# FNet mixing gated by a GLU on one Trainium2 core: three chunks of the sequence product together, and two of four block sums made by accumulating DMAs

## The chip, the cores and the metric

The kernel runs on one core of one Trainium2 chip. The metric is the device time of one execution in microseconds (us). The kernel before takes 804.07 us, the median of three runs (803.95 to 806.35). All operands are float32 in HBM (the chip's memory); work is done in SBUF (128 partitions) and in eight banks of PSUM.

## The reference

What is computed, cut to what matters; x is 2048 x 512, F is 1792:

```python
xn = layernorm(x)
s = C_re @ (xn @ H_re.T) - C_im @ (xn @ H_im.T)    # real part of a DFT along both axes
g = silu((sigmoid(xn @ w_gate) * (xn @ w_up)) @ w_down)
return x + s * g
```

C is the 2048 x 2048 DFT matrix of the sequence, H the 512 x 512 one of the hidden axis, each given as a real and an imaginary part.

## The kernel before

**Arithmetic.** Every float32 operand is split in two: ScalarE (ACT) copies a rounded high part (line 118), VectorE (DVE) subtracts it from the operand and keeps the low part (line 123). `mm3` (line 66) then makes one product of three matmuls: high by high, high by low, low by high. Each large product is done block-wise with seven products in place of eight, numbered k = 1 to 7; products 5, 6, 7 and 4 take sums of blocks as operands.

**Units.** The program is a list of units. One unit of the sequence product is 12 matmuls of 128 x 128 by 128 x 512. At unit n the main loop (last lines of the kernel) first calls what was put down with `sooner(n, ...)`, then issues the loads that units n to n+5 need (`LOAD_AHEAD`), then makes the high and low parts that units n to n+2 need (`SPLIT_AHEAD`), then records the unit's matmuls (`run`), and then calls what was put down with `after(n, ...)`. Nothing is reordered behind this: every engine gets its instructions in the order in which the program writes them.

**Queues.** All loads into SBUF are issued by SyncE (SP, line 79). All stores and all accumulating transfers are issued by GpSimd (POOL): `f_raw` (line 275, a finished block of the sequence product), `f_sum` (line 666, sums of such blocks), `g_part` (lines 479 and 482; line 479 accumulates in HBM), and `out`. Each queue starts its transfers in order; one instruction that waits holds up those behind it. A transfer is nearly always one page of 512 KB; SBUF holds 54 pages.

**The sequence stage.** The 2048 columns of the result fall into four chunks t of 512. In each chunk the contraction over the 2048 rows goes in four steps pp, so one product of one chunk is four units, and a chunk is 28 units; all four are 112 units (n = 112). On the x side the operands are blocks of the normalised x (`xs`, from `fetch`, `stats`, `normalise`) and sums of them (`a_sums`). `stats` runs two BN_STATS and two BN_AGGR on DVE, adds epsilon, and lets POOL take the power -1/2 (lines 164 to 173). On the DFT side each (t, pp) has four 512 KB blocks b11, b12, b21, b22 (the second index is the part, real or imaginary), and needs t1 = b11 + b12 for product 5, t2 = t1 + b22 for 6, t3 = b12 + b22 for 7 and t4 = t2 + b21 for 4. All four sums are made by DVE, in place (`onto`, `combine`, line 127), three units before their product; their blocks are loaded six units before it (`add_product`, line 308).

Chunks 0 and 1 go together through products 1 and 2: units 0 to 15 alternate between the two chunks, so that one block of x serves two units. Units 16 to 23 are chunk 2's products 1 and 2. Then come 5, 6, 7, 3, 4 of chunk 0 (units 24 to 43), of chunk 1 (44 to 63) and of chunk 2 (64 to 83), and chunk 3 as a whole (84 to 111). The sums of products grow in PSUM as chains "a", "b", "c" of two banks each (`CHAIN`); after product 1 its sum is copied by ACT into the banks of chain "b", and chain "a" goes on to products 6, 7 and 4.

**The start.** `begin` (line 349) records 12 matmuls on a tile of ones, loads the first block of x as two transfers of 256 KB, and makes the first operands by halves. For this first block alone the power is taken for each half as soon as its statistics are there (lines 167 and 168); for the others once per block (line 171).

**What else runs in the sequence stage.** `put_x` (line 699) lets POOL copy x into `out` (HBM to HBM), in units 40, 48, 56, ... ; `f_sums` (line 653) loads finished blocks of the first two chunks back, adds them on DVE and stores the sums, a first set from unit n-46 = 66 on and a second from n-35 = 77 on; `x_norm` and `x_ops` prepare the next stage.

Of the kernel before, what the change touches and what calls it, by code (L numbers as in the profile page):

```python
# [21 lines left out]
NT = S // 512  # L22
# [10 lines left out]
def fnet_glu_kernel(ctx: ExitStack, tc: tile.TileContext, x, x_t, c_re, c_im, w_h, w_gu, w_down, out):  # L33
# [112 lines left out]

    xs, mvs = {}, {}

    def fetch(j, pp, es=(0, 1)):
        if (j, pp) not in xs:  # L150
            xs[j, pp] = page([2, D], F32)
        rows = x[pp * SB : (pp + 1) * SB, :].rearrange("(p j e) d -> p j e d", j=2, e=2)[:, j]
        if len(es) == 2:
            nc.sync.dma_start(xs[j, pp], rows)
        else:
            nc.sync.dma_start(xs[j, pp][:, es[0], :], rows[:, es[0], :])

    def stats(j, pp):
        mv = stat.tile([P, 2, 2], F32, name="mv")
        rs = stat.tile([P, 2], F32, name="rs")  # L160
        mean, scale, bias = (moments[:, pp, m, j, :] for m in range(3))
        for e in range(2):
            st = stat.tile([P, 6], F32, name="st")
            nc.vector.bn_stats(st, xs[j, pp][:, e, :])
# [4 lines left out]
        if pp or j:  # L169
            nc.vector.tensor_scalar(rs, mv[:, :, 1], EPS, None, op0=ALU.add)  # L170
            nc.gpsimd.tensor_tensor(scale, rs, mhalf, op=ALU.pow)
        nc.vector.tensor_scalar(mean, mv[:, :, 0], -1.0, None, op0=ALU.mult)
        nc.gpsimd.tensor_tensor(bias, mean, scale, op=ALU.mult)
        return mv

# [50 lines left out]

    class Chunk:


        def __init__(self, t, tags, again):  # L230
            self.t, self.tags, self.ps, self.s = t, tags, {}, {}
            self.op, self.total = {}, {}
            for pp in range(4):
                b = {(j, m): c_block(t, pp, j, m) for j in range(2) for m in range(2)}
                self.op[1, pp] = Parts([b[0, 0]], b[0, 0].load, [2, SB])
                self.op[2, pp] = Parts([b[1, 0]], b[1, 0].load, [2, SB])
                if again:
# [16 lines left out]
        def needs(self, k, pp):  # L254
            return [aop[k, pp], self.op[k, pp]]

        def run(self, k, pp):
            ch = CHAIN[k]
# [4 lines left out]
            if (k, pp) == (1, 0) and self.t < 2:  # L263
                order.sort(key=lambda v: v[1])
            split_up = self.t < 2 and k in (1, 2) and (self.t, k, pp) != (0, 1, 0)
            for lows in ((0, 1), (2,)) if split_up else ((0, 1, 2),):
                for d, e in order:
                    ws = [v[:, e, d * P : (d + 1) * P] for v in wv]
                    first, last = k in (1, 5) and pp == e == 0, pp == 3 and e == 1
                    mm3(self.ps[ch, d], ws, [v[:, e, :] for v in xv], first, last, k not in (1, 5), self.t == 1, lows)  # L270
            if pp == 3:
                self.done(k)

# [43 lines left out]
    def begin_seq():  # L317
        tags = ("a", "b", "pd"), ("c", "pd", "a"), ("b", "pd", "a"), ("c", "a", "pd")
        chunks = [Chunk(t, dict(zip("abc", tags[t])), t in (1, 2)) for t in range(NT)]
        for i, k in enumerate((1, 2)):  # L320
            for pp in range(4):
                for c in chunks[:2]:
# [10 lines left out]
        for k in (1, 2):  # L333
            chunks[2].add_product(k)
        for pp in range(4):
            m = 9 + 2 * pp
            after(m, lambda pp=pp: a_sums(pp, (1,)))
            after(m + 1, lambda pp=pp: a_sums(pp, (3,)))
            after(m + 2, aop[5, pp].get)
            after(m + 3, lambda pp=pp: a_sums(pp, (2,)))  # L340
            after(m + 4, lambda pp=pp: a_sums(pp, (4,)))
        for c in chunks[:3]:
            for k in (5, 6, 7, 3, 4):
                c.add_product(k)
        for k in (1, 5, 6, 3, 7, 2, 4):
            chunks[3].add_product(k)
        return chunks

    def begin(chunks):
        for i, tag in enumerate(("gb", "ub", "pd", "pd")):  # L350
            idle = bank(tag)
            for _ in range((4, 4, 2, 2)[i]):
                nc.tensor.matmul(idle, ones[:, :P], ones, start=True, stop=True)
# [8 lines left out]
        for n in (2, 3):  # L362
            units[n][0][1].load()
        fetch(0, 2)
        for n in (4, 5):
            units[n][0][1].load()
        a = aop[1, 0]
        both = page([2, 2, D // 2])
        a.at = both[:, 0], both[:, 1]
        c.at = page([2, SB]), page([2, SB])  # L370
        first = a_block(0, 0, 0)

        def normed(e):
            scale = moments[:, 0, 1, 0, e : e + 1]
            nc.vector.tensor_scalar(first[:, e], first[:, e], mv[:, e, 0:1], scale, op0=SUB, op1=ALU.mult)

        def high(parts, src, e):
            nc.scalar.activation(parts[0][:, e], src[:, e], AF.Copy)

        def low(parts, src, e):  # L380
            nc.vector.tensor_tensor(parts[1][:, e], src[:, e], parts[0][:, e].bitcast(F32), op=SUB)

        mv = stats(0, 0)
        high(c.at, raw.at, 0)
        normed(0)
        high(a.at, first, 0)
        low(c.at, raw.at, 0)
        low(a.at, first, 0)
        high(c.at, raw.at, 1)
        normed(1)  # L390
        high(a.at, first, 1)
        low(c.at, raw.at, 1)
        low(a.at, first, 1)
        units[1][0][1].high()
        stats(0, 1)
        units[1][0][1].get()
        units[2][0][1].get()
        normalise(0, 1, d=0)
        aop[1, 1].get()
        for pp in range(2):  # L400
            after(4 + pp, lambda pp=pp: normalise(0, pp, d=1))


    XK = {(0, 0): 1, (1, 0): 2, (0, 1): 0, (1, 1): 3}
# [420 lines left out]
    with tc.manual_schedule():  # L825
# [97 lines left out]
```

## Time and profile before

| | |
|---|---|
| median of three runs | 804.07 us |
| the profiled execution | 804.23 us |
| its span, first to last instruction | 802.4 us |
| granted TensorE clock, mean | 0.996 |
| PE (matmuls) busy | 790.3 us, 3468 instructions |
| DVE busy | 685.9 us, 894 instructions |
| ACT busy | 510.7 us, 776 instructions |
| POOL busy | 123.0 us, 162 instructions |
| moved by DMA | 174.72 MB, mean 218 GB/s |

How to read it: the span is what the profiler saw of one execution; the 1.8 us between it and the execution's time lie outside. Busy times are sums over instructions; an engine with 98% busy time is the one that sets the end, unless its instructions are slowed down. DMA shares are shares of the core's 16 DMA engines together. The granted clock tells which part of its full speed TensorE was allowed.

### The profile page before, as it was taken

The page shows a single profiled execution, that of the slowest core. Times are in us where ns is not written, and L with a number is a line of the kernel's source. Part 1 is how long each engine was busy: PE and PEld are TensorE (multiplying, and loading weights), DVE is VectorE, ACT ScalarE, POOL GpSimd, SP SyncE. Part 2 cuts the span into 40 slices and gives each one's busy share as a digit, 9 for nine tenths or more (in the row PEclk, how much of TensorE's full clock was granted, in tenths as well). Part 3 has the DMA queues.
Part 4 walks back from the last instruction along what each step waited for, and adds up shares of the span by engine and source line. Part 5 has one row for each costly group of instructions (what it writes and reads, how often), then busy time and mean ns, then how long its engine had stood idle before and what let it go on. Part 6 is the DMA issues. An engine that isn't in the chain of part 4 may idle for free.

```text
span 802.4 us, 9870 instructions
## 1 busy us (share of the span) xinstructions
PE 790.3 (98%) x3468; PEld 651.6 (81%) x3468; DVE 685.9 (85%) x894; ACT 510.7 (64%) x776; POOL 123.0 (15%) x162
## 2 busy tenths in 40 slices
PE   7999999999999999999999999999999999999997
PEld 5888888888878888888887887888888888888885
DVE  6898999878899798899999967869688898896956
ACT  4984565525434555677777866666577787888471
POOL 2430001000110000001211111222131111112201
PEclk9999999999999999999999999999999999999999
DMA  8954057297898335238976976799999798999996
GB/s 339 410 192 160 27 179 267 86 340 256 283 374 366 105 110 202 83 115 214 202 131 97 179 166 184 245 275 240 241 261 213 159 227 227 223 290 299 298 340 106
DMA packets 49329, 174.72 MB, mean 218 GB/s; under 512 B 5504, under 2 KB 5760, under 8 KB 49280
## 3 DMA queue, kind: packets, MB, share of 16 engines
q0 software_dynamic: 20320, 70.28, 39.8%
q1 hardware_dynamic: 28880, 103.76, 35.5%
q8 instruction: 27, 0.44, 0.2%
q14 instruction: 22, 0.18, 0.1%
q10 hardware_dynamic: 80, 0.07, 0.0%
HBM read 106.95 MB, written 70.80 MB: 222 GB/s over the span
## 4 chain that ended last, share of the span: by engine, by line
PE 85%; DVE 5%; DMA 4%; issue 4%; POOL 1%; ACT 1%; SPq 0%; POOLq 0%; ACTq 0%; DVEq 0%
PE pd L70 25%; PE ga L70 15%; PE ua L70 15%; PE gc L70 10%; PE uc L70 10%; PE gb L70 5%; PE ub L70 5%; DMA g_part<-page 2%; DVE page L127 2%; DVE page L123 1%; DMA page<-in_x_dram 1%; DMA f_raw<-page 1%; POOL g_part L479 1%; ACT page L118 0%; DVE page L574 0%
## 5 line engine op out<-in xcount | busy, mean ns | idle before, releaser
L123 DVE TENSOR_TENSOR page<-page 128x512 fp32r<-128x512 f32 (+1 forms) x384 | 348.8, 938 | 62.9 <-ACT page L118 60.8
L118 ACT ACTIVATE page<-page 128x512 fp32r<-128x512 f32 (+1 forms) x384 | 303.1, 829 | 148.3 <-DVE page L127 116.5
L70 PE MATMUL pd<-page 128*128 128x512 f32 (+1 forms) x984 | 238.3, 386 | 0.0
L70 PEld LDWEIGHTS pd<-page 128*128 128x128 f32 x984 | 183.2, 188 | 37.5
L127 DVE TENSOR_TENSOR page<-page 128x1024 f32<-128x1024 f32 (+2 forms) x252 | 204.7, 833 | 4.9 <-DMA page<-in_w_gu_dram 3.8
L70 PE MATMUL ga<-page 128*128 128x512 f32 x600 | 154.4, 391 | 4.3 <-ACT page L118 1.8
L70 PE MATMUL ua<-page 128*128 128x512 f32 x600 | 154.2, 391 | 0.0
L70 PEld LDWEIGHTS ga<-page 128*128 128x128 f32 x600 | 112.5, 188 | 30.3 <-ACT page L118 2.4
L70 PEld LDWEIGHTS ua<-page 128*128 128x128 f32 x600 | 113.3, 189 | 23.7
L479 POOL DMA_DIRECT2D g_part<-page x76 | 66.4, 874 | 275.8 <-ACT page L488 159.0
L70 PE MATMUL gc<-page 128*128 128x512 f32 x384 | 98.6, 389 | 0.0
L70 PE MATMUL uc<-page 128*128 128x512 f32 x384 | 98.4, 389 | 0.0
L488 ACT ACTIVATE page<-pd 128x512 f32<-128x512 f32 x140 | 81.7, 600 | 24.3 <-PE pd L70 17.0
L70 PEld LDWEIGHTS gc<-page 128*128 128x128 f32 x384 | 72.2, 188 | 15.5 <-DVE page L123 0.5
L70 PEld LDWEIGHTS uc<-page 128*128 128x128 f32 x384 | 72.1, 188 | 14.9
L70 PE MATMUL gb<-page 128*128 128x512 f32 x252 | 64.9, 390 | 0.4 <-DVE page L123 0.4
L70 PE MATMUL ub<-page 128*128 128x512 f32 x252 | 64.6, 389 | 0.0
L70 PEld LDWEIGHTS gb<-page 128*128 128x128 f32 x252 | 47.2, 188 | 10.6 <-DVE page L123 0.8
L70 PEld LDWEIGHTS ub<-page 128*128 128x128 f32 x252 | 47.3, 188 | 9.8
L275 POOL DMA_DIRECT2D f_raw<-page x16 | 8.7, 544 | 220.6 <-DVE page L287 146.8
L614 DVE TENSOR_TENSOR page<-page 128x512 f32<-128x512 f32 x28 | 19.3, 689 | 8.7 <-ACT page L611 7.9
L574 DVE TENSOR_TENSOR page<-page,pd 128x512 f32<-128x512 f32 x28 | 18.5, 684 | 6.9 <-PE pd L70 6.9
(90 smaller groups left out, 347.8 us busy)
## 6 DMA issues: line engine op xcount, KB each, us to landing
g_part<-page POOLq DMA_DIRECT2D x84, 512.0 KB, 6.7
page<-in_c_re_dram SPq DMA_DIRECT2D x48, 512.0 KB, 7.7
page<-in_c_im_dram SPq DMA_DIRECT2D x32, 512.0 KB, 6.2
page<-f_raw SPq DMA_DIRECT2D x28, 512.0 KB, 8.2
page<-in_w_gu_dram SPq DMA_DIRECT2D x22, 512.0 KB, 5.9
f_raw<-page POOLq DMA_DIRECT2D x16, 512.0 KB, 5.7
f_sum<-page POOLq DMA_DIRECT2D x16, 512.0 KB, 7.1
page<-f_sum SPq DMA_DIRECT2D x16, 512.0 KB, 12.4
```

The lines of the kernel that those rows point to most:

```text
L70: nc.tensor.matmul(ps, ws[w], ms[m], start=first and i == 0, stop=last and i == 2, skip_group_check=go_on)
L118: nc.scalar.activation(self.parts[0], self.raw, AF.Copy)
L123: nc.vector.tensor_tensor(lo, self.raw, hi.bitcast(F32), op=SUB)
L127: (engine or nc.vector).tensor_tensor(dst, a, b, op=op)
L275: nc.gpsimd.dma_start(f_raw[self.t][block], v)
L479: nc.gpsimd.dma_start(g_part[i], pg, accum_op=ADD)
L488: nc.scalar.activation(pg[:, o, :], po, AF.Copy, scale=float(sign))
L574: nc.vector.tensor_add(self.part[:, o, :], self.part[:, o, :], ps)
L614: nc.vector.tensor_mul(s[k][:, 0, :], s[k][:, 0, :], ps["u" + tag] if tag else s[k][:, 1, :])
```

## The change

- **Three chunks together** (`TOGETHER = 3`): units 0 to 23 alternate between chunks 0, 1 and 2, so that one block of x serves three units. Products 1 and 2 of these chunks share a chain "p"; product 1 is copied from PSUM to SBUF, and copied back two units before product 6 (`again`). `fetch`, `stats`, `normalise` and `a_sums` get new places to match. In all of these units the three passes of `mm3` run one after the other over the four (d, e), where before the first two went together.
- **t1 and t3 by DMA** (`Sum`): SP loads the first block into a page, and an accumulating DMA that POOL issues adds the second block in SBUF. Both are issued nine units before the product. A page that t1 was made in before held b11, which product 1 (chunks 0 and 3) could share; now it is a load of its own, and b12 is read twice. t2 and t4 stay with DVE, loaded six units ahead.
- **Powers by halves**: the first two blocks of x are prepared by halves (`prepare`): DVE adds epsilon for each half and POOL takes the power of it. The first block of x is loaded in one transfer. Three more matmuls on the tile of ones.
- **f_sums(0, 1)** from unit n-26 = 86 on, instead of n-35 = 77.

The transfers of DFT blocks go from 80 to 124: 92 plain ones of SP and 32 accumulating ones of POOL. By groups of eight units, in the order of issue (from the code):

| units | 0-7 | 8-15 | 16-23 | 24-31 | 32-39 | 40-47 | 48-55 | 56-63 | 64-71 | 72-79 | 80-87 | 88-95 | 96-103 |
|---|---|---|---|---|---|---|---|---|---|---|---|---|---|
| before, plain | 13 | 8 | 9 | 2 | 4 | 8 | 2 | 12 | 2 | 5 | 9 | 2 | 4 |
| after, plain | 13 | 9 | 9 | 5 | 8 | 8 | 3 | 8 | 5 | 6 | 8 | 6 | 4 |
| after, accumulating | 0 | 1 | 4 | 3 | 4 | 4 | 1 | 4 | 3 | 1 | 3 | 4 | 0 |

Cut to its core, the diff reads:

```diff
@@ stats @@
-            if pp == j == 0:
-                nc.gpsimd.tensor_scalar(rs[:, e : e + 1], mv[:, e, 1:2], EPS, None, op0=ALU.add)
+            if apart:
+                nc.vector.tensor_scalar(rs[:, e : e + 1], mv[:, e, 1:2], EPS, None, op0=ALU.add)
                 nc.gpsimd.tensor_tensor(scale[:, e : e + 1], rs[:, e : e + 1], mhalf[:, e : e + 1], op=ALU.pow)
...
+    class Sum(Load):
+        def __init__(self, a, b, shape):
+            super().__init__(a, shape)
+            self.more = b
+        def load(self):
+            if self.at is None:
+                super().load()
+                nc.gpsimd.dma_start(self.at, self.more, accum_op=ADD)
+            return self.at
+        get = load
...
+    TOGETHER = 3
@@ Chunk.__init__ @@
                 if again:
-                    b[0, 0], b[1, 0] = c_block(t, pp, 0, 0), c_block(t, pp, 1, 0)
-                b11, b12, b21, b22 = b[0, 0], b[0, 1], b[1, 0], b[1, 1]
-                t1 = Value([b11, b12], onto(b11.load, b12.load))
+                    b[1, 0] = c_block(t, pp, 1, 0)
+                b21, b22 = b[1, 0], b[1, 1]
+                t1 = Sum(c_re[t, 0, pp], c_im[t, 0, pp], [2, SB])
+                t3 = Sum(c_im[t, 0, pp], c_im[t, 1, pp], [2, SB])
                 t2 = Value([b22], onto(t1.get, b22.load))
-                t3 = Value([b22], onto(b12.load, b22.load))
@@ Chunk.run @@
-            split_up = self.t < 2 and k in (1, 2) and (self.t, k, pp) != (0, 1, 0)
-            for lows in ((0, 1), (2,)) if split_up else ((0, 1, 2),):
+            split_up = self.t < TOGETHER and k in (1, 2)
+            for lows in ((0,), (1,), (2,)) if split_up else ((0, 1, 2),):
@@ Chunk.done @@
-            if k == 1:
+            if k < 3 and self.t < TOGETHER:
+                v = self.snap(f"p{k}", "p")
+                if k == 2:
+                    self.put(0, v)
+            elif k == 1:
@@ add_product @@
-        def add_product(self, k, total=(6, 3)):
+        def add_product(self, k):
+            total = (9, 3) if k in (5, 7) else (6, 3)
             for pp in range(4):
                 m = len(units)
+                if (k, pp) == (6, 0) and self.t < TOGETHER:
+                    after(m - 2, self.again)
@@ begin_seq @@
-                m = 8 * i + 2 * pp
-                if m > 4:
-                    sooner(m - (6, 7)[i], lambda i=i, pp=pp: fetch(i, pp))
-                if m > 2:
-                    sooner(m - (4, 5)[i], lambda i=i, pp=pp: stats(i, pp))
-                    sooner(m - 2, units[m][0][1].get)
-                    sooner(m - 2, lambda i=i, pp=pp: normalise(i, pp))
+                m = TOGETHER * (4 * i + pp)
+                if i:
+                    sooner(m - 11, lambda pp=pp: fetch(1, pp))
+                    after(m - 8, lambda pp=pp: stats(1, pp))
+                    sooner(m - 5, lambda pp=pp: normalise(1, pp))
+                else:
+                    if pp > 1:
+                        after(m - 5, lambda pp=pp: stats(0, pp))
+                        sooner(m - 2, lambda pp=pp: normalise(0, pp, 0))
...
@@ begin @@
-            for _ in range((4, 4, 2, 2)[i]):
+            for _ in range((4, 4, 4, 3)[i]):
...
-        for e in range(2):
-            fetch(0, 0, (e,))
+        fetch(0, 0)
...
-        f_sums(0, 1, n - 35, 2)
+        f_sums(0, 1, n - 26, 2)
```

How it moves instructions, at two places. The first is POOL's queue where the finished blocks of chunk 2 are stored (`f_raw_99`, `f_raw_98`, `f_raw_97`; units 75, 79 and 83). Before, the rows there are these; `f_sum` are the stores of f_sums, `out_dram<-in_x_t_dram` those of put_x:

```order
L275 DMA f_raw_99<-page 128x1024
L666 DMA f_sum_108<-page 128x1024
L275 DMA f_raw_98<-page 128x1024
L666 DMA f_sum_109<-page 128x1024
L701 DMA out_dram<-in_x_t_dram 128x2x512
L666 DMA f_sum_110<-page 128x1024
L275 DMA f_raw_97<-page 128x1024
```

And now, where `page<-in_c_im_dram` at line 227 is the accumulating transfer of a `Sum` (here for chunk 3's product 5):

```order
L296 DMA f_raw_99<-page 128x1024
L227 DMA page<-in_c_im_dram 128x1024
L296 DMA f_raw_98<-page 128x1024
L227 DMA page<-in_c_im_dram 128x1024
L736 DMA out_dram<-in_x_t_dram 128x2x512
L227 DMA page<-in_c_im_dram 128x1024 x2
L296 DMA f_raw_97<-page 128x1024
L701 DMA f_sum_108<-page 128x1024
L701 DMA f_sum_109<-page 128x1024
```

The accumulating transfers stand behind stores that wait for a product's result, and the f_sum stores of the second set have moved behind the last store of chunk 2.

The second place is DVE's order in the first units, where low parts (line 123) alternate with the statistics of the next block of x. Before:

```order
L123 TENSOR_TENSOR page<-page 128x512
L164 BN_STATS st<-page 128x6
L165 BN_AGGR mv<-st 128x2
L164 BN_STATS st<-page 128x6
L165 BN_AGGR mv<-st 128x2
L170 TENSOR_SCALAR rs<-mv 128x2
L172 TENSOR_SCALAR moments<-mv 128x2
L123 TENSOR_TENSOR page<-page 128x1024 x2
```

And now, behind unit 4, where the statistics of two blocks meet:

```order
L160 BN_STATS st<-page 128x6
L161 BN_AGGR mv<-st 128x2
L166 TENSOR_SCALAR rs<-mv 128x2
L170 TENSOR_SCALAR moments<-mv 128x2
L160 BN_STATS st<-page 128x6
L161 BN_AGGR mv<-st 128x2
L160 BN_STATS st<-page 128x6
L161 BN_AGGR mv<-st 128x2
L166 TENSOR_SCALAR rs<-mv 128x2
L170 TENSOR_SCALAR moments<-mv 128x2
L123 TENSOR_TENSOR page<-page 128x1024 x2
```

Two blocks' statistics now stand together ahead of the low parts, where before one block's did.

More of the change, by code (lines that the diff above doesn't have):

```diff
@@ L147, in fnet_glu_kernel, with fetch, stats @@
     xs, mvs = {}, {}
-    def fetch(j, pp, es=(0, 1)):
-        if (j, pp) not in xs:
-            xs[j, pp] = page([2, D], F32)
+    def fetch(j, pp):
+        xs[j, pp] = page([2, D], F32)
         rows = x[pp * SB : (pp + 1) * SB, :].rearrange("(p j e) d -> p j e d", j=2, e=2)[:, j]
[L153 to L158, printed above, removed]
+        nc.sync.dma_start(xs[j, pp], rows)
+    def stats(j, pp, apart=None):
         mv = stat.tile([P, 2, 2], F32, name="mv")
@@ L165, in stats @@
             nc.vector.bn_aggr(mv[:, e, :], st)
-            if pp == j == 0:
-                nc.gpsimd.tensor_scalar(rs[:, e : e + 1], mv[:, e, 1:2], EPS, None, op0=ALU.add)
+            if apart:
+                nc.vector.tensor_scalar(rs[:, e : e + 1], mv[:, e, 1:2], EPS, None, op0=ALU.add)
                 nc.gpsimd.tensor_tensor(scale[:, e : e + 1], rs[:, e : e + 1], mhalf[:, e : e + 1], op=ALU.pow)
-        if pp or j:
+        if not apart:
             nc.vector.tensor_scalar(rs, mv[:, :, 1], EPS, None, op0=ALU.add)
             nc.gpsimd.tensor_tensor(scale, rs, mhalf, op=ALU.pow)
+        if apart:
+            apart(mv, 0)
         nc.vector.tensor_scalar(mean, mv[:, :, 0], -1.0, None, op0=ALU.mult)
+        if apart:
+            apart(mv, 1)
         nc.gpsimd.tensor_tensor(bias, mean, scale, op=ALU.mult)
@@ L255, in needs, with again @@
             return [aop[k, pp], self.op[k, pp]]
+        def again(self):
+            self.chain("a")
+            for d in range(2):
+                nc.scalar.activation(self.ps["a", d], self.s["p1"][:, d, :], AF.Copy)
         def run(self, k, pp):
-            ch = CHAIN[k]
+            ch = "p" if k < 3 and self.t < TOGETHER else CHAIN[k]
             if k in (1, 5) and pp == 0:
@@ L262, in run @@
             order = [(d, e) for d in range(2) for e in range(2)]
[L263 removed]
+            if (k, pp) == (1, 0) and self.t < TOGETHER:
                 order.sort(key=lambda v: v[1])
[L265 to L266 removed]
+            split_up = self.t < TOGETHER and k in (1, 2)
+            for lows in ((0,), (1,), (2,)) if split_up else ((0, 1, 2),):
                 for d, e in order:
@@ L269, in run @@
                     first, last = k in (1, 5) and pp == e == 0, pp == 3 and e == 1
-                    mm3(self.ps[ch, d], ws, [v[:, e, :] for v in xv], first, last, k not in (1, 5), self.t == 1, lows)
+                    mm3(self.ps[ch, d], ws, [v[:, e, :] for v in xv], first, last, k not in (1, 5), self.t > 0 or (k < 3 and pp > 0), lows)
             if pp == 3:
@@ L317, in begin_seq @@
     def begin_seq():
-        tags = ("a", "b", "pd"), ("c", "pd", "a"), ("b", "pd", "a"), ("c", "a", "pd")
-        chunks = [Chunk(t, dict(zip("abc", tags[t])), t in (1, 2)) for t in range(NT)]
+        tags = {"p": "a", "c": "pd", "a": "a"}, {"p": "b", "c": "b", "a": "c"}, {"p": "c", "c": "pd", "a": "a"}, {"a": "c", "b": "a", "c": "pd"}
+        chunks = [Chunk(t, tags[t], t < TOGETHER) for t in range(NT)]
         for i, k in enumerate((1, 2)):
             for pp in range(4):
-                for c in chunks[:2]:
+                for c in chunks[:TOGETHER]:
@@ L331, in begin_seq @@
                 if i:
                     after(m + 2, lambda pp=pp: store_moments(pp))
-        for k in (1, 2):
-            chunks[2].add_product(k)
         for pp in range(4):
[L336 to L341, printed above, removed]
+            m = 4 * TOGETHER + TOGETHER * pp
@@ L342, in begin_seq @@
+            after(m - 3, lambda pp=pp: a_sums(pp, (1,)))
+            after(m - 2, lambda pp=pp: a_sums(pp, (3,)))
+            after(m - 1, aop[5, pp].get)
+            after(m + 1, lambda pp=pp: a_sums(pp, (2,)))
+            after(m + 5 + 2 * pp, lambda pp=pp: a_sums(pp, (4,)))
         for c in chunks[:3]:
@@ L361, in begin, with tile_of @@
         fetch(0, 1)
-        for n in (2, 3):
+        for n in (2, 3, 4):
             units[n][0][1].load()
         fetch(0, 2)
-        for n in (4, 5):
+        for n in (5,):
             units[n][0][1].load()
-        a = aop[1, 0]
-        both = page([2, 2, D // 2])
-        a.at = both[:, 0], both[:, 1]
         c.at = page([2, SB]), page([2, SB])
[L371 to L375, printed above, removed]
+        def tile_of(pp):
+            a = aop[1, pp]
+            both = page([2, 2, D // 2])
+            a.at = both[:, 0], both[:, 1]
+            return a.at, a_block(0, 0, pp)
@@ L377, in high, with normed, low @@
+        def normed(pp, mv, e):
+            v = a_block(0, 0, pp)[:, e]
+            nc.vector.tensor_scalar(v, v, mv[:, e, 0:1], moments[:, pp, 1, 0, e : e + 1], op0=SUB, op1=ALU.mult)
         def high(parts, src, e):
             nc.scalar.activation(parts[0][:, e], src[:, e], AF.Copy)
-        def low(parts, src, e):
+        def low(parts, src, e=slice(0, 2)):
             nc.vector.tensor_tensor(parts[1][:, e], src[:, e], parts[0][:, e].bitcast(F32), op=SUB)
-        mv = stats(0, 0)
-        high(c.at, raw.at, 0)
@@ L385, in begin, with prepare, step @@
[L385 to L395, printed above, removed]
+        def prepare(pp, between):
+            parts, src = tile_of(pp)
+            def step(mv, e):
+                normed(pp, mv, e)
+                high(parts, src, e)
+                between(e)
+            stats(0, pp, step)
+            return parts, src
@@ L396, in begin @@
+        high(c.at, raw.at, 0)
+        a, first = prepare(0, lambda e: high(c.at, raw.at, 1) if e == 0 else None)
+        for e in range(2):
+            low(c.at, raw.at, e)
+            low(a, first, e)
         units[1][0][1].get()
+        units[2][0][1].high()
+        a, second = prepare(1, lambda e: None)
+        units[3][0][1].high()
         units[2][0][1].get()
[L398 to L401, printed above, removed]
+        low(a, second)
```

3 lines of the change are left out of this document (added).

## The prediction

> **What bounds the kernel now.** I read the totals first, then the chain of work that ended last, then PE's waits, then the start and the stretch of the sequence stage row by row. Busy times by engine, and the chain's shares:
>
> ```profile
> span 802.4 us, 9870 instructions
> PE 790.3 (98%) x3468; PEld 651.6 (81%) x3468; DVE 685.9 (85%) x894; ACT 510.7 (64%) x776; POOL 123.0 (15%) x162
> PE 85%; DVE 5%; DMA 4%; issue 4%; POOL 1%; ACT 1%; SPq 0%; POOLq 0%; ACTq 0%; DVEq 0%
> ```
>
> PE is busy nearly always. The change adds three warm-up matmuls and takes no product away, so it can gain only what PE waits or runs slowly. These are all of PE's waits (us in total, times, longest):
>
> ```profile
> PE ga L70 <- ACT page L118: 1.8, 1, 1.8
> PE gb L353 <- DVE ones L50: 1.4, 1, 1.4
> PE ga L70 <- ACT page L378: 1.4, 1, 1.4
> PE ga L70 <- ACT page L596: 1.1, 2, 0.6
> PE gb L70 <- DVE page L123: 0.4, 1, 0.4
> ```
>
> Two lie at the start (L378, L118 at 1.8), L596 is in a later stage, and in the sequence stage beyond the start only 0.4 us remains, for DVE. Next the pace, from two rows of the chain of waits (start, duration):
>
> ```profile
> 37.59 2.72 PE pd L70 x12
> 67.50 21.76 PE pd L70 x96
> ```
>
> A unit of 12 matmuls takes 2.72 us. At 37.59 nine units are done, and 37.59 - 9 x 2.72 = 13.1; at 67.50 it is twenty, and 67.50 - 20 x 2.72 = 13.1 again. **So the start costs 13.1 us and from then on PE runs at its pace.** The start itself, in the timeline (start, duration, what, in brackets the wait ahead of it):
>
> ```profile
> 1.45 2.08 PE L353 MATMUL gb<-ones 128*128 128x512 f32 x4 [1.45 <-DVE ones L50]
> 5.03 1.91 PE L353 MATMUL pd<-ones 128*128 128x512 f32 x4
> 8.35 1.29 PE L70 MATMUL ga<-page 128*128 128x512 f32 x3 [1.42 <-ACT page L378]
> 12.40 1.68 POOL L171 TENSOR_TENSOR moments<-rs,mhalf 128x2 f32<-128x2 f32 x1 [4.18 <-DVE moments L172]
> 14.74 1.09 ACT L179 ACTIVATE page<-page,moments 128x256 f32<-128x256 f32 x2 [2.06 <-POOL moments L173]
> 16.54 1.25 PE L70 MATMUL ga<-page 128*128 128x512 f32 x4 [1.78 <-ACT page L118]
> ```
>
> The first product starts at 8.35. With two units per block of x, the second block is wanted at 8.35 + 2 x 2.72 = 13.8; its statistics, POOL's power and ACT's normalisation bring it at 16.54. One more thing costs here, the granted clock (busy time of PE, PEld, DVE, ACT, POOL, then clock, DMA share, GB/s):
>
> ```profile
> 17.00:21.00 4.00, 4.00 (x13) 3.10 (x12) 3.90 (x9) 1.39 (x2) 1.81 (x2) 0.57 1.03 420
> ```
>
> In these 4 us right behind the wait of 1.8 us the clock is 0.57: 4 x (1 - 0.57) = 1.7 us lost.
>
> **The change, part by part.**
>
> *32 DVE adds go.* Such an add, and the four stretches in which they lie:
>
> ```profile
> L127 DVE TENSOR_TENSOR page<-page 128x1024 f32<-128x1024 f32 x92 | 111.5, 1218 | 0.2 <-DMA page<-in_c_im_dram 0.2
> 60.00:110.00 50.00, 50.00 (x223) 41.39 (x222) 46.39 (x49) 31.50 (x42) 0.54 (x1) 1.00 0.25 84
> 110.00:160.00 50.00, 50.00 (x222) 41.42 (x221) 46.15 (x46) 24.62 (x30) 3.08 (x5) 1.00 0.56 203
> 160.00:200.00 40.00, 40.00 (x178) 33.10 (x178) 32.33 (x31) 14.96 (x17) 3.64 (x6) 1.00 0.84 302
> 200.00:227.00 27.00, 27.00 (x121) 22.36 (x120) 24.72 (x23) 11.13 (x12) 2.88 (x5) 1.00 0.79 275
> ```
>
> 32 x 1.218 = 39 us of DVE go. PE was busy in every microsecond of these rows, so this is worth nothing on the path; at most the 0.4 us of the one DVE wait.
>
> *The start.* Warm-ups: 12 take from 1.45 to 5.03 + 1.91 = 6.94, so 0.457 each; 15 end at 1.45 + 15 x 0.457 = 8.3. The first product cannot start before 8.35 either way, so they cost nothing. With three units per block the second block is wanted at 8.35 + 3 x 2.72 = 16.5 where 16.54 was reached before, and its power now goes by halves: **the 1.8 us wait goes, and with it the 1.7 us of slow clock**. What is late next: DVE. Its rows:
>
> ```profile
> 21.00:60.00 39.00, 39.00 (x173) 32.14 (x172) 36.65 (x65) 34.49 (x49) 14.67 (x17) 1.00 0.80 298
> L164 DVE BATCH_NORM_STATS2 st<-page 128x6 f32<-128x512 f32 x16 | 10.8, 677 | 3.8 <-DMA page<-in_x_dram 3.7
> L123 DVE TENSOR_TENSOR page<-page 128x1024 fp32r<-128x1024 f32 x182 | 219.4, 1218 | 34.0 <-ACT page L118 33.5
> L171 POOL TENSOR_TENSOR moments<-rs,mhalf 128x2 f32<-128x2 f32 x7 | 10.7, 1529 | 21.1 <-DVE moments L172 21.1
> ```
>
> DVE is busy 36.65 of 39 us there without holding PE. After the change two blocks' statistics stand together behind unit 4 (4 x 0.68 us and the small steps, estimated at half as much again: 4.1 us), ahead of low parts that are wanted two units later. Bounds for PE's wait there: 0 and 4.1; I take 1.2, since the lead of 5.4 us covers most of it. The blocks of units 9 to 16 need ACT and POOL's 1.53 us power in turn: 0 to 2.4, I take 1.2. The first unit, whose halves now come from one load, is stretched by 0.5 (0 to 1). Sum: 8.35 + 0.5 + 1.2 + 1.2 = 11.25 in place of 13.1, **a gain of 1.85 us**; by the bounds from 4.7 gained (nothing waits) to 2.7 lost, and a renewed slow clock would add 1.7.
>
> *What an accumulating transfer costs.* The traces show none into SBUF; the nearest row is g_part, which accumulates in HBM. The two queues, and what stands in them:
>
> ```profile
> q0 software_dynamic: 20320, 70.28, 39.8%
> q1 hardware_dynamic: 28880, 103.76, 35.5%
> L479 POOL DMA_DIRECT2D g_part<-page x76 | 66.4, 874 | 275.8 <-ACT page L488 159.0
> out_dram<-page POOLq DMA_DIRECT2D x7, 512.0 KB, 10.3
> 227.00:258.00 31.00, 30.62 (x135) 25.00 (x134) 30.18 (x28) 13.38 (x15) 4.64 (x8) 1.00 1.02 417
> ```
>
> At 0.524 MB a page q1 has 198 plain pages: 0.355 x 802.4 / 198 = 1.44 us of all 16 engines each. q0 has 134, of which 76 + 7 = 83 accumulate: (0.398 x 802.4 - 51 x 1.44) / 83 = 2.96 us each, 2.06 times a plain one. Where the engines are full (417 GB/s in the last row) a plain page takes 0.524 / 0.417 = 1.26 us, so 2.06 times that is 2.58. An add in SBUF may be cheaper: the lower bound is a plain page, 1.26; the upper 2.96. I take 2.58, nearest to the row.
>
> [...]
>
> *Where there is room for it.* Chunk 0's and 1's sixteen accumulating transfers and their extra loads fall into 60 to 160, where the DMA share is 0.25 and 0.56: 37.5 + 22 = 59 us free, against 16 x 2.58 = 41 and some 9 plain ones, 11 us. They fit. From 160 to 258 (units 54 to 90) the free time is 40 x 0.16 + 27 x 0.21 + 0 = 12.1 us. There the sum is, from the table by units: accumulating +12 (4 + 3 + 1 + 3 and one), plain ones unchanged (29 and 29), and of f_sums' second set two of its eight transfers move behind 258 (2.5 us). **12 x 2.58 - 12.1 - 2.5 = 16.4 us more work than room at 258.** What of it is covered:
>
> ```profile
> DMA to landing us min/median/max: 3.2/3.3/3.4
> 258.00:285.00 27.00, 27.00 (x121) 22.36 (x120) 22.45 (x21) 13.78 (x16) 0.00 (x0) 1.00 0.25 84
> ```
>
> The first row is SP's loads from 258 to 285, when the queues are empty: 3.3 us. Blocks for t2, t4 are loaded six units ahead, 16.3 us, so the cover is 16.3 - 3.3 = 13.0 us; the accumulating ones have more, 24.5 less their own time. So PE waits about **16.4 - 13.0 = 3.4 us**, around 255 to 275; after that the engines are 75% free and it is caught up. In order on POOL's queue, stores of finished blocks stand ahead of the accumulating ones, and f_sum's stores behind: nothing but the later f_sums waits for these. On DVE, t2's and t4's adds are queued ahead of low parts: a late load stops DVE and by it PE. That is the way in which the lack shows. By the bounds of the price, 12 x 1.26 leaves 0.5 us and no wait; 12 x 2.96 leaves 20.9 and a wait of 7.9.
>
> *The rest.* b11's extra loads are in the table. p1's copies to SBUF and back are ACT's (9 more instructions; ACT has 64% busy), hidden behind PE; cost nothing unless the chain is wanted within one unit, and `again` stands two units ahead.
>
> **Sum.** 804.23 (the profiled execution) - 1.85 + 3.4 = **805.8 us**; the median of the runs is 0.16 lower than that execution, which changes nothing.
>
> **The rivals.**
>
> A, the forecast: the start gains, the full DMA engines take it back. 805.8, own range 804 to 809.
>
> B: the accumulating transfers stay hidden. For it: SBUF is not HBM, and the cover of 13.0 us is lost only above (13.0 + 12.1 + 2.5) / 12 = 2.3 us each. Against it: the 2.58. Time: 804.23 - 1.85 = 802.4.
>
> C, slower: the price is 2.96 and the backlog decides. From 2.3 us on, each 0.1 us costs 1.2 us of waiting; at 2.96 it is 7.9 us, and as such a wait is longer than the 1.8 us behind which the clock fell to 0.57, it falls again: + 1.7. Time: 804.23 - 1.85 + 7.9 + 1.7 = 812.0. For it: 227 to 258 is already full at 1.02. Against it: the engines took 2.06 times, not 2.35.
>
> [...]
>
> D, slower: the start loses. The two statistics in a row hold PE for the whole 4.1 us and ACT's turn for 2.4, a wait over 1.8 us brings the slow clock: 8.35 + 0.5 + 4.1 + 2.4 + 1.7 = 17.1 in place of 13.1, with the transfers hidden 808.2. Against it: DVE at 36.65 of 39 held nobody.
>
> **How the numbers follow.** A 0.47, B 0.30, C 0.15, D 0.08. A measurement of this kernel can tell about 0.3%, 2.4 us. Same (801.7 to 806.5): three fifths of A, two thirds of B, 0.48. Faster: the rest of B and a start near its better bound, 0.14. Slower: the rest of A, C and D, 0.38. The range runs from below B, with a start that gains 3 us (801.2), to C (812.0); one tenth is left out on each side.
>
> **What will show it.** First unit at 8.35, no wait of 1.8 us ahead of the second block, granted clock 1.0 from 17 to 21, and 11.3 us lost when the pace is reached. DMA share near 1 from 160 to 270 in place of 0.84 and 0.79; PE's waits for L123 between 250 and 275, with DVE's L127 waiting for page<-in_c loads ahead of them. Wrong would be: free DMA time left in 200 to 227 (price too high), waits of PE at 60 to 160 (an engine other than these), or waits in the hidden stage, where no edit reaches.

## The result, and the profile after

The changed kernel takes 815.6 us, median of five runs (812.97 to 816.44), against 803.95 for the kernel before in the same session. The ratio is 1.0139, with a 95% interval of 1.0125 to 1.0154: **slower by 1.4%**. The forecast was 805.8 with a range up to 812.0. The profiled execution took 812.97 us, the quickest of the five, so what the trace shows is the least of the harm.

The totals after, and the two DMA queues:

```profile
span 811.2 us, 9964 instructions
PE 793.0 (98%) x3471; PEld 652.5 (80%) x3471; DVE 651.7 (80%) x867; ACT 512.0 (63%) x785; POOL 146.6 (18%) x193
q0 software_dynamic: 24928, 87.06, 50.0%
q1 hardware_dynamic: 30464, 110.05, 36.1%
```

DVE has lost 34 us of work, and the span has grown by 8.8. GpSimd's queue q0 went from 39.8% to 50.0%. PE's waits after (us in total, times, longest; those of the first products and of the later stage left out):

```profile
PE ga L70 <- DVE page L123: 4.8, 1, 4.8
PE pd L70 <- DVE page L123: 2.6, 1, 2.6
...
PE gb L70 <- DVE page L123: 1.2, 2, 0.8
```

Before, PE waited 0.4 us for DVE in the whole sequence stage; now it is two long waits and some at the start. By stretches (busy time of PE, PEld, DVE, ACT, POOL, then granted clock, DMA share, GB/s):

```profile
17.00:21.00 4.00, 4.00 (x19) 3.34 (x18) 3.90 (x9) 2.14 (x4) 1.37 (x1) 1.00 1.03 422
21.00:60.00 39.00, 37.43 (x160) 29.24 (x160) 31.70 (x56) 29.73 (x44) 12.84 (x17) 1.00 0.76 306
60.00:75.00 15.00, 15.00 (x68) 12.43 (x67) 13.76 (x18) 9.37 (x14) 3.33 (x5) 1.00 1.01 233
75.00:110.00 35.00, 35.00 (x156) 29.00 (x155) 28.80 (x33) 25.86 (x37) 5.94 (x8) 1.00 0.86 255
110.00:160.00 50.00, 50.00 (x222) 41.39 (x222) 37.55 (x37) 25.59 (x31) 10.04 (x13) 1.00 0.95 293
160.00:200.00 40.00, 40.00 (x178) 33.15 (x177) 26.03 (x25) 15.58 (x18) 7.79 (x11) 1.00 0.99 306
200.00:227.00 27.00, 22.23 (x89) 17.93 (x89) 15.18 (x15) 10.25 (x11) 3.95 (x7) 0.87 0.96 299
227.00:258.00 31.00, 31.00 (x138) 25.68 (x137) 23.00 (x21) 11.81 (x13) 5.74 (x8) 1.00 1.04 337
258.00:285.00 27.00, 24.42 (x102) 19.79 (x101) 22.79 (x20) 10.68 (x14) 6.36 (x9) 0.94 1.03 380
285.00:300.00 15.00, 15.00 (x68) 12.40 (x67) 10.51 (x10) 8.18 (x9) 0.56 (x1) 1.00 1.00 303
```

Read the DMA share first. Before, it was 0.25 from 60 to 110 and then, in the same stretches as here, 0.56, 0.84, 0.79, 1.02, 0.25 and 0.41; now it is 0.86 to 1.04 all the way from 60 to 300. Then PE: it is idle 1.57 us from 21 to 60 (the start), 4.77 from 200 to 227 and 2.58 from 258 to 285. Behind both of the later waits the clock is low (start, length, then the same columns):

```profile
218.50:223.00 4.50, 4.20 (x10) 3.33 (x11) 4.50 (x5) 3.90 (x4) 1.24 (x2) 0.50 0.71 218
264.00:268.00 4.00, 3.55 (x9) 2.85 (x10) 4.00 (x5) 0.00 (x0) 0.12 (x1) 0.57 1.03 421
```

That costs 4.5 x 0.50 = 2.2 us and 4 x 0.43 = 1.7 us more. **The two stops together take about 4.8 + 2.2 + 2.6 + 1.7 = 11.3 us.** The chain of waits agrees: unit 92, the first of a new product, starts there at 273.85, and 273.85 - 92 x 2.72 - 12.3 (lost at the start, next) = 11.3.

The start, from the row of the chain of waits that begins with unit 24:

```profile
77.58 10.88 PE pd L70 x48
```

77.58 - 24 x 2.72 = 12.3 us are lost before the pace is reached, 0.8 less than the 13.1 that the same view gave before.

What held PE in the two stops is told by DVE's waits and by the chain. DVE's two waits, first of the stretch 200 to 220, then of 226 to 266:

```profile
DVE page L123 <- DMA f_sum<-page: 9.4, 1, 9.4
...
DVE page L127 <- DMA page<-f_raw: 7.7, 1, 7.7
```

And the three longest links of the chain of waits from 180 to 270 (start, duration; a DMA from its issue to its landing):

```profile
188.69 14.90 DMA page<-in_c_im_dram
...
204.68 12.76 DMA f_sum<-page
...
240.74 21.20 DMA page<-f_raw
```

The first stop: a load of SP, the first block of a t3 (it comes from `in_c_im`), takes 14.9 us; its accumulating transfer waits 3.9 us for it at the head of POOL's queue; the f_sum store behind that starts at 204.68 and takes 12.8 us; and DVE, by the releaser that the profile names, waits 9.4 us for the landing of the store before it writes a low part (line 123). It waits for a store, so what it needs is the page that the store reads. The second stop: f_sums' load of a finished block, issued 240.74, takes 21.2 us, and DVE's add (line 127) waits 7.7 us for it, with low parts queued behind. In both cases the transfer that lands last belongs to f_sums. In the first stop another was nearly as late: the accumulated block of the stopped unit was sent for at 199.38 and landed 12.1 us later, and ACT waited 2.7 us for it before it could make the high part; PE stopped at 218.80 - 4.77 = 214.0.

### The profile page after: what moved, and what is told of

The parts are those of the page before. It is cut to its first block, busy times and chain, and to the rows that moved or that the text cites. A ratio compares the mean times of both kernels' runs of the same rounds, so it can differ in the third digit from the quotient of the medians.

```text
span 811.2 us, 9964 instructions
## 1 busy us (share of the span) xinstructions
PE 793.0 (98%) x3471; PEld 652.5 (80%) x3471; DVE 651.7 (80%) x867; ACT 512.0 (63%) x785; POOL 146.6 (18%) x193
## 4 chain that ended last, share of the span: by engine, by line
PE 84%; DMA 9%; DVE 2%; ACT 2%; issue 1%; POOL 1%; SPq 0%; DVEq 0%; POOLq 0%
PE pd L70 26%; PE ga L70 14%; PE ua L70 14%; PE uc L70 10%; PE gc L70 10%; PE gb L70 5%; PE ub L70 5%; DMA page<-in_c_re_dram 3%; DMA page<-f_raw 3%; DMA page<-in_c_im_dram 2%; DMA f_sum<-page 2%; ACT page L118 1%; DVE page L123 1%; ACT page L179 1%; POOL moments L167 0%
## 5 line engine op out<-in xcount | busy, mean ns | idle before, releaser
L123 DVE TENSOR_TENSOR page<-page 128x1024 fp32r<-128x1024 f32 (+1 forms) x383 | 346.8, 939 | 95.4 <-ACT page L118 80.6
L118 ACT ACTIVATE page<-page 128x1024 fp32r<-128x1024 f32 (+1 forms) x383 | 301.0, 830 | 139.4 <-DVE page L127 103.1
L127 DVE TENSOR_TENSOR page<-page 128x512 f32<-128x512 f32 (+2 forms) x220 | 165.8, 777 | 10.5 <-DMA page<-f_raw 7.7
L70 PE MATMUL gc<-page 128*128 128x512 f32 x408 | 106.6, 389 | 0.0
L70 PE MATMUL uc<-page 128*128 128x512 f32 x408 | 106.6, 389 | 0.0
L70 PEld LDWEIGHTS gc<-page 128*128 128x128 f32 x408 | 76.6, 188 | 15.9
L70 PEld LDWEIGHTS uc<-page 128*128 128x128 f32 x408 | 76.6, 188 | 15.9
L70 PEld LDWEIGHTS gb<-page 128*128 128x128 f32 x228 | 42.6, 188 | 10.9 <-DVE page L123 2.2
L70 PEld LDWEIGHTS ub<-page 128*128 128x128 f32 x228 | 42.8, 188 | 8.9
L227 POOL DMA_DIRECT2D page<-in_c_im_dram x32 | 28.3, 931 | 94.5 <-DMA page<-in_c_re_dram 25.2
## 6 DMA issues: line engine op xcount, KB each, us to landing
page<-f_raw SPq DMA_DIRECT2D x28, 512.0 KB, 11.3
```

Source lines behind the costliest of these rows:

```text
L70: nc.tensor.matmul(ps, ws[w], ms[m], start=first and i == 0, stop=last and i == 2, skip_group_check=go_on)
L118: nc.scalar.activation(self.parts[0], self.raw, AF.Copy)
L123: nc.vector.tensor_tensor(lo, self.raw, hi.bitcast(F32), op=SUB)
L127: (engine or nc.vector).tensor_tensor(dst, a, b, op=op)
L227: nc.gpsimd.dma_start(self.at, self.more, accum_op=ADD)
```

## The experiments

Three theories were set against each other. Theory 1: f_sums decides, because its loads are issued only three units (8.2 us) ahead. Theory 2: the DMA engines have more work than room, because an accumulating transfer holds them about twice as long as a plain one (1.94 times, as measured below); what is late first is an accident. Theory 3: POOL's queue decides, because an accumulating transfer waits for its first block (38.1 us of POOL's waits for loads ahead of line 227 in the changed kernel) and holds the stores behind it. All comparisons are with the kernel before, run again beside each.

### t1 and t3 by DVE again, all else as changed

```diff
-                    b[1, 0] = c_block(t, pp, 1, 0)
-                b21, b22 = b[1, 0], b[1, 1]
-                t1 = Sum(c_re[t, 0, pp], c_im[t, 0, pp], [2, SB])
-                t3 = Sum(c_im[t, 0, pp], c_im[t, 1, pp], [2, SB])
+                    b[0, 0], b[1, 0] = c_block(t, pp, 0, 0), c_block(t, pp, 1, 0)
+                b11, b12, b21, b22 = b[0, 0], b[0, 1], b[1, 0], b[1, 1]
+                t1 = Value([b11, b12], onto(b11.load, b12.load))
+                t3 = Value([b22], onto(b12.load, b22.load))
...
-            total = (9, 3) if k in (5, 7) else (6, 3)
+            total = (6, 3)
```

> The changed kernel with t1 and t3 made by DVE again, loaded six units ahead as before; the three chunks together, the powers by halves, the warm-ups and the later f_sums stay. If the accumulating transfers are the cause (theories 1, 2 and 3 below alike), PE's two stops at units 74 and 89 (7.0 and 4.3 us with the slow clock behind them) go and the start's gain of 0.8 us stays: 803.2. If three chunks together are the cause, the stops stay: 812 to 816.

803.5 us; ratio 0.9989 [0.9980, 0.9999]. The stops are gone; the rows where the changed kernel stopped, in this run:

```profile
200.00:227.00 27.00, 27.00 (x121) 22.36 (x120) 24.62 (x24) 11.69 (x13) 2.88 (x5) 1.00 0.80 281
258.00:285.00 27.00, 26.78 (x118) 21.85 (x117) 25.72 (x23) 14.30 (x16) 2.28 (x4) 1.00 0.47 156
```

So the accumulating transfers, with the loads that come with them, are the harm, and all the rest of the change together gains a tenth of a per cent.

### Only the accumulating transfers, in the kernel before

```diff
...
-                t1 = Value([b11, b12], onto(b11.load, b12.load))
+                t1 = Sum(c_re[t, 0, pp], c_im[t, 0, pp], [2, SB])
+                t3 = Sum(c_im[t, 0, pp], c_im[t, 1, pp], [2, SB])
...
-                t3 = Value([b22], onto(b12.load, b22.load))
...
-        def add_product(self, k, total=(6, 3)):
+        def add_product(self, k):
+            total = (9, 3) if k in (5, 7) else (6, 3)
```

> The kernel before with t1 and t3 by SP's load and the accumulating DMA nine units ahead, and nothing else of the change: two chunks together, start and f_sums as before. Theories 1 and 2 expect PE stops of 8 to 12 us between 200 and 280: 812 to 816; with f_sums' second set earlier (from unit 77) the stops come earlier and rather longer. If three chunks together are needed for the harm, 804.

816.02 us; ratio 1.0152 [1.0127, 1.0177]. This one edit does as much harm as the whole change. PE's waits for DVE after the start are here 3.4 and 1.8 us and some smaller ones; three chunks together are not needed for it.

### The same transfers without the add

The second transfer of a `Sum` becomes plain; it overwrites the first block, so t1 and t3 are not sums here.

```diff
-                nc.gpsimd.dma_start(self.at, self.more, accum_op=ADD)
+                nc.gpsimd.dma_start(self.at, self.more)
```

> The changed kernel with the accumulating transfers as plain ones: same queue, same waits, same bytes, but the second block overwrites the first, so t1 and t3 are not sums. Theory 1 (f_sums: its loads, three units ahead on a full DMA, stop DVE) and theory 2 (the price of the add on the DMA engines) expect 32 x (2.69 - 1.26) = 46 us less DMA work and no stop: 803 to 805. Theory 3 (POOL's queue: an accumulating transfer waits for its first block and holds the stores behind it) expects the stops as they are: 811 to 816.

803.58 us; ratio 0.9986 [0.9976, 0.9996]. The number of transfers, their queue, their order and their waits are those of the changed kernel, and no stop is left: the add itself is what harms. **Theory 3 falls**, as an explanation by itself. The stretch where the changed kernel stopped, in this run:

```profile
160.00:200.00 40.00, 40.00 (x179) 33.10 (x178) 27.89 (x27) 16.68 (x21) 6.25 (x11) 1.00 0.96 348
200.00:227.00 27.00, 27.00 (x121) 22.37 (x120) 20.27 (x20) 11.31 (x12) 3.92 (x7) 1.00 0.97 328
227.00:258.00 31.00, 31.00 (x138) 25.67 (x137) 22.89 (x21) 12.08 (x14) 5.19 (x10) 1.00 1.02 407
258.00:285.00 27.00, 27.00 (x120) 22.21 (x119) 22.87 (x22) 16.00 (x18) 3.75 (x7) 1.00 0.85 341
```

The shares are nearly as high, 0.96, 0.97 and 1.02, and PE is busy throughout. So a share near 1 is not by itself the harm; what the add costs on top is measured next.

### The price of the add by itself

Two runs of the kernel before with eight unused pages in the quiet stretch: a plain load of SP, and into the same page an accumulating or a plain transfer of POOL.

```diff
...
+        for i in range(8):
+            sooner(20 + 2 * i, Sum(c_re[3, 0, 0], c_im[3, 0, 0], [2, SB]).load)
```

> The kernel before with eight more pages that nothing uses, one every second unit from unit 20: a plain load of SP and an accumulating transfer of POOL into it, in the quiet stretch. It measures the price by itself. Before, the DMA engines were busy 0.25 x 50 = 12.5 us from 60 to 110; with a price of 2.58 (the forecast) they are busy about 12.5 + 8 x 1.3 + 8 x 2.58 = 43.5, with 2.96 about 46.6, with the cost of a plain transfer 33. No effect on the time if the units lie in the quiet stretch: 804.

> The same with eight plain transfers of POOL in place of the accumulating ones: 12.5 + 16 x 1.3 = 33 us busy from 60 to 110 by every theory. The difference between the two runs over eight is what the add costs on top of a plain transfer: 1.3 by the forecast's price, 1.2 by the totals of the changed kernel and its plain variant, 0 if the add is free in the quiet. The time 804.

The times were 803.56 and 803.23 us, beside 802.95 for the kernel before, one run each: next to nothing on the path. The row from 55 to 120, which holds all sixteen transfers, first of the kernel before:

```profile
55.00:120.00 65.00, 65.00 (x289) 53.81 (x288) 60.72 (x66) 39.00 (x52) 3.09 (x6) 1.00 0.40 134
```

with eight plain ones of POOL:

```profile
55.00:120.00 65.00, 65.00 (x288) 53.81 (x288) 60.74 (x66) 38.94 (x52) 7.28 (x14) 1.00 0.74 264
```

and with eight accumulating ones:

```profile
55.00:120.00 65.00, 65.00 (x288) 53.84 (x287) 60.70 (x66) 38.90 (x52) 10.00 (x14) 1.00 0.90 258
```

A plain page costs (0.74 - 0.40) x 65 / 16 = 1.38 us of all engines, the add (0.90 - 0.74) x 65 / 8 = 1.30 us on top: **2.68 us for an accumulating transfer into SBUF, 1.94 times a plain one.** The totals say nearly the same: q0 takes 46.0% of 800.7 us in the run with the second transfers plain and 50.0% of 811.2 in the changed kernel, 37.3 us for 32, or 1.17 each on top. From 60 to 110 the expected 43.5 us came out as 0.91 x 50 = 45.5, and the 33 of the plain run as 0.69 x 50 = 34.5.

### Loads of f_sums six and nine units ahead

```diff
...
-        f_sums(0, 0, n - 46, 2)
-        f_sums(0, 1, n - 26, 2)
+        f_sums(0, 0, n - 46, 2, 6)
+        f_sums(0, 1, n - 26, 2, 9)
```

The last argument is the lead of its loads, which was three.

> The changed kernel with the blocks for f_sums loaded six and nine units ahead of their adds instead of three; no transfer more or less. Theory 1 expects the second stop (4.3 us with the slow clock behind it, DVE's add waiting for a block that takes 21.2 us to land) to go: 4 us faster than the changed kernel, about 811.5. Theory 2 expects another late block in its place and 814 to 817. On the first stop, where a page is held by a store of f_sums, both expect little change.

812.96 us; ratio 1.0106 [1.0089, 1.0123], by the two ratios 0.3% better than the changed kernel, some 2.6 us. This time lies between what the theories expected, 811.5 by theory 1 and 814 to 817 by theory 2, and does not decide; the trace does. The first stop is nearly as long and comes earlier; the chain there reads:

```profile
184.97 6.87 DMA page<-in_c_im_dram
...
193.02 12.04 DMA f_raw<-page
...
205.14 1.06 ACT page L118
```

Now it is the store of a finished block that holds a page, and ACT's high part (line 118) that waits. The second stop breaks into pieces:

```profile
200.00:227.00 27.00, 22.89 (x93) 18.11 (x92) 15.21 (x14) 11.02 (x12) 4.30 (x7) 0.94 0.99 316
227.00:258.00 31.00, 29.44 (x129) 23.80 (x128) 20.51 (x20) 11.27 (x12) 5.14 (x7) 1.00 1.03 352
258.00:285.00 27.00, 25.97 (x113) 20.59 (x112) 24.52 (x22) 12.34 (x16) 6.39 (x9) 1.00 1.03 362
```

PE is idle 4.11 + 1.56 + 1.03 = 6.7 us in these rows, against 4.77 + 2.58 = 7.4 in the changed kernel; the rest of the gain goes with the clock, which was slow for less time (0.94 and 1.00 from 200 to 227 and from 258 to 285, in place of 0.87 and 0.94). In one of the pieces DVE's add waits 1.5 us for a block from `in_c_im`, loaded by SP, which takes 22.9 us to land: the sort of wait that the prediction had in mind. So **theory 1 falls in its strict form**: with f_sums served early, other transfers take its place, as theory 2 says.

### f_sums in other places

Its second set back at unit 77, as before the change:

```diff
-        f_sums(0, 1, n - 26, 2)
+        f_sums(0, 1, n - 35, 2)
```

> The changed kernel with the second set of f_sums back at unit 77. No transfer more or less. Theory 2 (the add's price fills the DMA engines from 60 to 300 us; whichever transfer is then wanted soonest stops DVE) expects the second stop earlier and no smaller: 813 to 818. Theory 1 (the cover of the f_sums loads decides, wherever the engines are full) expects the same here.

816.33 us; ratio 1.0152 [1.0128, 1.0176]. The stops stay (5.2 and 2.3 us of waiting for line 123), the second 11 us earlier. Both theories expected as much, so this run does not part them; the place of f_sums within the full stretch matters little.

Both early sets out of the stretch:

```diff
-        f_sums(0, 0, n - 46, 2)
-        f_sums(0, 1, n - 26, 2)
+        f_sums(0, 0, n + 4, 2)
+        f_sums(0, 1, n + 14, 2)
```

> The changed kernel with both early sets of f_sums moved out of the full stretch, to units 116 and 126 (330 us on, where the DMA share is low). The 32 accumulating transfers stay. Theory 2 by its budget: the plain variant needed 119 us of engine time from 160 to 285, the adds bring 16 x 1.17 = 19 us more, the f_sums moved out take 16 x 1.3 = 21 us away: 117 of 125, no stop, 803 to 805. Theory 1 expects the same, since the loads with short cover are gone; but if other loads stop DVE the time stays above 808 and both fall.

808.24 us; ratio 1.0049 [1.0035, 1.0063]. No stop, but not the 803 to 805 that both theories expected; the rows of this run where the changed kernel stopped, and the one where f_sums now runs:

```profile
200.00:227.00 27.00, 27.00 (x121) 22.36 (x120) 16.77 (x17) 11.16 (x13) 1.46 (x2) 1.00 0.80 251
227.00:258.00 31.00, 31.00 (x139) 25.66 (x138) 21.58 (x20) 12.81 (x15) 5.01 (x7) 1.00 1.04 345
258.00:285.00 27.00, 27.00 (x121) 22.36 (x120) 19.65 (x19) 15.28 (x18) 3.47 (x4) 1.00 0.79 229
...
300.00:360.00 60.00, 57.87 (x253) 46.93 (x252) 55.07 (x75) 34.59 (x56) 4.80 (x9) 1.00 0.58 206
```

With 16 transfers fewer in the stretch PE is never idle there, as the budget of theory 2 had it. Most of the gain is given back later: PE waits 3.8 us in all for line 631 of ACT, against 0.5 in the changed kernel, and 1.9 of it lies between 300 and 360, where f_sums now runs. That the moved f_sums cause these later waits is likely by their place; it was not tried.

### Half of the accumulating transfers

t1 by DMA, t3 by DVE with a load of b12 of its own.

```diff
...
-                t3 = Sum(c_im[t, 0, pp], c_im[t, 1, pp], [2, SB])
+                t3 = Value([b12, b22], onto(b12.load, b22.load))
...
```

> The changed kernel with t1 by DMA and t3 by DVE: 16 accumulating transfers instead of 32. Theory 2 by its budget expects about 119 - 8 x 0.4 + 8 x 1.17 = 125 us from 160 to 285, at the edge: stops of 0 to 3 us in place of 11, 803 to 806. If the harm were in proportion to the number of accumulating transfers: half of 11.3, 808.5.

808.98 us; ratio 1.0057 [1.0044, 1.0071]. The budget of theory 2, 803 to 806, was too kind; the 808.5 of a harm in proportion to the number of accumulating transfers is nearer. One stop of some size is left, in the second place, and its cause is the old one:

```profile
DVE page L127 <- DMA page<-f_raw: 7.7, 1, 7.7
...
PE pd L70 <- DVE page L123: 2.8, 1, 2.8
```

With half of the adds it is again f_sums' load, whose cover is three units, that comes late first. So the two theories meet, as I read it: the add's price fills the engines, and the transfers with the least cover decide how much of it PE feels.

### The start alone, mended

With the sums by DVE, the statistics and the normalisation of the second half's blocks one unit later each, so that no two blocks' statistics stand together.

```diff
...
-                    after(m - 8, lambda pp=pp: stats(1, pp))
-                    sooner(m - 5, lambda pp=pp: normalise(1, pp))
+                    after(m - 7, lambda pp=pp: stats(1, pp))
+                    sooner(m - 4, lambda pp=pp: normalise(1, pp))
```

> The changed kernel with t1 and t3 by DVE, and at the start the statistics of the second half's blocks one unit later and their normalisation one unit later, so that two blocks' statistics no longer stand together on DVE and ACT does not wait for POOL's power. If the order on DVE and ACT is what holds PE at units 7 to 20 (3.1 us), 1 to 2 us less than with the sums by DVE alone: 801.5 to 802.5. If the loads of x are what is late there, no change: 803.5.

**801.54 us; ratio 0.9966 [0.9954, 0.9979]: faster than both kernels.** From 21 to 60 PE is now never idle, where the changed kernel idled 1.57 us, and from 60 to 300 DVE, with the adds back, holds PE for no more than 0.2 us:

```profile
21.00:60.00 39.00, 39.00 (x170) 31.32 (x169) 32.74 (x58) 31.17 (x45) 12.94 (x15) 1.00 0.90 355
60.00:300.00 240.00, 239.78 (x1055) 197.08 (x1054) 221.93 (x216) 123.50 (x148) 17.47 (x30) 1.00 0.63 222
```

## Why the prediction was wrong, point by point

- **The DVE adds are worth nothing on the path: right.** With them back PE loses 0.2 us in 240 (last row above).
- **The start gains 1.85 us: it gained 0.8.** The 1.8 us wait and the slow clock of 17 to 21 went, as said (clock 1.00 there). What was late next was on DVE and ACT, as said too, but I took 0.5 + 1.2 + 1.2 = 2.9 us behind the first product for it, and 12.3 - 8.35 leaves nearly 4. The mended start shows that the order on DVE and ACT is the cause: with the sums by DVE the row of the chain that begins with unit 24 starts at 77.80 (12.5 us lost), and with that order changed as well at 75.22 (9.9 us lost).
- **An accumulating transfer costs 2.58 us: right, 2.68 measured.** The nearest row, in HBM, told the price in SBUF within 4%, and part of that is luck: the ratio is 1.94 in place of 2.06 and a plain page 1.38 us in place of 1.26, and the two errors cancel.
- **From 60 to 160 they fit: right**; shares of 0.86 to 1.01, no wait.
- **16.4 us more work than room, less 13.0 us of cover, leaves 3.4: this step failed, and in the cover.** "Blocks for t2, t4 are loaded six units ahead, 16.3 us, so the cover is 16.3 - 3.3 = 13.0 us", and of POOL's stores "nothing but the later f_sums waits for these". The changed kernel shows neither of its stops at a load for t2 or t4, and only the second where the forecast had its one, at 255 to 275. The stops show a store of f_sums (12.8 us) that keeps a page from DVE, and a load of f_sums whose cover is 8.2 - 3.3 = 4.9 us by the same working. With 4.9 in place of 13.0 the same sum gives 11.5 us where 4.8 + 2.6 = 7.4 of waiting was measured; so the 11.5 is of the right order of size, but too large. A part of the difference is that low parts are made two units, 5.4 us, ahead: DVE's waits of 9.4 and 7.7 us came through to PE as 4.8 and 2.6. Nor did the accumulating transfers keep the "24.5 less their own time" that the prediction gave them: the one of the first stop was sent for at 199.38, 14.7 us before PE wanted it.
- **The clock.** The forecast had it in rivals C and D alone; both waits brought it (0.50 and 0.57 behind them), 3.9 us together. That any wait over 1.8 us brings it, as C and D took it, no run shows: behind the 2.8 us of the run with half of the accumulating transfers the clock stayed at 1.00. The sum with the measured terms: 804.23 - 0.8 + 11.3 = 814.7 for an execution that took 812.97; where the remaining 1.7 lies was only read, not tried: the wait of 0.4 us for line 123 in the kernel before is gone, and that for ACT in the later stage is 0.5 in place of 1.1 us; these make 1.0, and 0.7 stays open.
- **Rival C** had the right kind of harm, waits behind the full DMA engines with a slow clock after them, and nearly the size (812.0), but by a price of 2.96, where 2.68 was measured, and with the cover of 13.0; that it came near is luck. It had 0.15.

What stays open is how much of the first stop is due to the number of pages. That DVE (9.4 us) and ACT (6.2 us) waited for stores of f_sums to land says that pages were short; more than 54 were not tried.

## What to carry to other kernels

The accumulating DMA was not a free adder here: it moved 39 us of work from an engine that held nobody to the DMA engines, at nearly the price of a second transfer each (1.30 us of all engines for the add, 1.38 for a plain page). When you weigh such a change, add up DMA engine time by stretches, and then look for the transfer with the *least* cover in the full stretch, stores that hold pages included; the cover of the transfers that you are changing is not enough. A part that turns out harmless, as the grouping by three does here, is found by taking the sum apart; the start was worth more than the sums.

## What the runs showed of the hardware

The clock fell behind a wait of PE of 1.8 us (to 0.57, the kernel before), of 4.8 and of 2.6 us (to 0.50 and 0.57, after), but not behind one of 2.8 us in the run with half of the accumulating transfers, where the wait ends at 258 and the clock is 1.00 (same columns as above):

```profile
255.00:258.00 3.00, 0.21 (x1) 0.00 (x0) 2.36 (x3) 0.00 (x0) 0.55 (x1) 1.00 1.03 421
258.00:262.00 4.00, 3.95 (x17) 3.26 (x18) 4.00 (x4) 0.00 (x0) 0.29 (x1) 1.00 1.02 419
```

So the length of a wait alone does not tell. What else decides was not shown.

Transfers took far longer to land where the DMA engines were full: f_sums' load of 512 KB took 21.2 us in the changed kernel (DMA share 1.04 there), where SP's loads from 258 to 285 in the kernel before (share 0.25) took 3.3 us.
